# One matmul chain for group 1, its loads' issuers and the start's filler matmuls rearranged in an S5 and MLP kernel

## The chip, the cores and the metric

The kernel runs on one core of a Trainium2 chip. The metric is the device time of one execution in microseconds (us), as the median of several runs. The engines are named as in the profile: PE (TensorE), PEld (its weight loads), ACT (ScalarE), DVE (VectorE), POOL (GpSimd) and SP (SyncE, which issues DMAs).

## The reference

x is 2048 rows of 448 columns in bf16. A layer norm of x feeds two branches: a diagonal complex state space model (S5), and an MLP behind a second layer norm, whose silu gates the first.

```python
xn = layernorm(x)
# S5: 448 complex states, one recurrence over the 2048 rows
Lam_bar = exp(dt * Lam);  B_bar = ((Lam_bar - 1) / Lam)[:, None] * B
Bu = xn @ B_bar.T
for t in range(2048):
    h = Lam_bar * h + Bu[t]          # hs[t] = h
s = 2 * real(hs @ C.T) + xn * Dskip
# MLP 448 -> 1792 -> 448
m = gelu(layernorm(xn) @ w1 + b1) @ w2 + b2
out = x + s * silu(m)
```

## The kernel before

The rows are worked in four groups of 512. For each group the kernel makes both norms, transposes them by DMA (`xn` to `xnT`, `xn2` to `xn2T`), forms the MLP's first product with w1 (`mm1_phase`, matmuls of L662, gelus of L668 on ACT into `gT`), its second with w2 (`mm2`, L784 and L787, silu of L790), the state inputs (`bu_phase`, L691: rows are taken in pairs, so each group has 256 columns of two rows), the scan of the states (`ssm`, L740 to L769, with the scans themselves at L750, the states of odd and even rows in `hx` and `hz`), the output of the state space model (`yt`, L806 to L829), and the sum that is written out (`out_dma`, or `out_pe` for the last group). Group 0 also makes its tables: decay powers in `WT`, the scaled B and C matrices (`BT`, `CQ`, `CZ`; L596, L597).

Nothing is issued where it is written. Each operation is recorded as a task with the keys that it reads and writes; `link()` derives what it must wait for from the order in which the tasks are written; `emit()` then issues all tasks in the order of a list of numbers, ORDER (L154). Each engine works through its own instructions in that order, and waits on semaphores. Some tasks have two forms, for two engines (a copy on ACT or DVE, a small operation on POOL or DVE, a row of a norm on DVE or ACT, the four numbers of a norm's scale on POOL or DVE: ten DVE instructions L423 to L433, or five POOL ones with a power): a second list, SECOND (L174), names the tasks that take the second form.

The written order, from which the dependencies come, is a string of words, STEPS (L180). `m1211` is the first product (m) of group 1, tile pair 2, on bank pair 1, second phase (1); a tile pair is two times 128 of the 1792 columns, phase 0 takes three quarters of its depth, phase 1 the rest, and the gelus follow phase 1. `b0031` is a state input of group 0, job 0, bank pair 3, stage 1. `W` is a tile of the second product, `S` a scan, `Y` an output, `L` and `N` norms, `G` and `U` the gelu and the silu table's load on ACT (L466). The bank pairs of PSUM are 0 and 1, 2 and 3, 4 and 7, 5 and 6.

At the start, x, w1 (four chunks, each a main part of three times 128 rows and a remainder of 64 rows, `ldw1`), B and w2 are loaded by SP's queue, the parameters of the states and b1 by ACT's. PE runs filler matmuls on constants (`dummies`, L378) between its first small matmuls, then turns b1 and the skip row into columns (L549, L555), and begins group 0's first product (L662), which runs in halves of 256 columns. The product needs `xn2T` of group 0, whose halves come from PE transposes (L407) by copies (L301), and the w1 chunk with its remainder; the copy of the 64 rows at L301 or L302 within `w1_sb` is needed by a second phase.

Of the kernel before, what the change touches and what calls it, by code (L numbers as in the profile page):

```python
# [148 lines left out]
def dram_ap(t, offset, ap):  # L149
    return bass.AP(tensor=t.tensor, offset=offset, ap=ap)  # L150
# [1 line left out]


ORDER = [int(k) for k in """  # L154
# [18 lines left out]
""".split()]  # L173
SECOND = [int(k) for k in """  # L174
26 29 32 56 60 69 83 90 113 115 172 173 175 177 178 180 181 182 202 204 205 207 208 209 210 212 214 216 218 220 222 234 236 238 240 244 246 256 258
270 277 278 280 324 338 349 360 361 364 365 409 443 444 445 446 471 472 473 474 475 487 489 527 528 529 542 549 551 560 575
""".split()]


STEPS = """  # L180
L1 N1 W006 W015 W022 W033 G1 m1000 m1120 m1001 m1210 m1121 m1300 m1211 m1301 m1410 b0030 m1500 b0120 m1411 b0031 b0121 m1501 b0032 m1610 b0122 m1611
b0033 b0123 U1 L2 S0 W130 W101 W112 W123 G2 m2000 m2110 b1020 m2001 m2111 b1130 m2200 b1021 m2310 m2201 b1131 m2311 m2400 b1022 m2510 b1132 m2401
m2511 b1023 m2600 b1133 m2601 U2 L3 Y03d2 Y00d3 Y01d4 Y02d7 O0 N2 S1 W205 W216 W220 W231 Y13d2 Y10d3 Y11d4 Y12d7 O1 N3 G3 m3000 b2030 m3110 b2120
m3001 b2031 m3111 b2121 m3200 b2032 m3310 b2122 m3201 b2033 m3311 b2123 S2 m3400 b3030 m3510 b3120 m3401 b3031 b3121 m3511 b3032 m3600 b3122 m3601
# [13 lines left out]
def bass_recurrent_scan__ssm_conv_s5__mixer_channel_mlp__prompt_kernel(  # L198
# [11 lines left out]
    L, D, F = 2048, 448, 1792  # L210
# [6 lines left out]
    with ExitStack() as es:  # L217
        def SB(name, shape, dtype=BF):
            return es.enter_context(nc.sbuf_tensor(name, shape, dtype))
# [12 lines left out]
        w1_sb = SB("w1_sb", [128, 4, F])  # L232
# [9 lines left out]
        drows = vrows[64:66, 64:512]  # L242
# [54 lines left out]
        def pe(fn, reads=(), writes=(), split=False):  # L297
            kb.add("pe", fn, reads, writes, split=split)

        def copy(pairs, rd, wr):  # L300
            kb.either(("act", [lambda e, o=o, i=i: e.activation(o, i, ACT.Copy) for o, i in pairs]),  # L301
                      ("dve", [lambda e, o=o, i=i: e.tensor_copy(o, i) for o, i in pairs]), rd, wr)  # L302

        with nc.Block():
# [17 lines left out]
            def ld(eng, o, i, writes, reads=()):  # L322
                kb.dma(eng, o, i, reads=reads, writes=writes)
# [4 lines left out]
            def ldx(b0, n, reads=()):  # L328
                ld("sp", x_all[:, b0:b0 + n, :, :], dram_ap(A_x, b0 * 256 * D, [[2 * D, 128], [256 * D, n], [D, 2], [1, D]]),
                   [f"x{b}" for b in range(b0, b0 + n)], reads)  # L330
# [4 lines left out]
            def ldw1(c):  # L335
                a, w = CH[c][0] * 128, CH[c][1] * 128
                ld("sp", w1_sb[:, 0:3, a:a + w], dram_ap(B_w1, a, [[F, 128], [128 * F, 3], [1, w]]), [f"w1_{c}"])
                ld("sp", w1_sb[64:128, 3, a:a + w], dram_ap(B_w1, 384 * F + a, [[F, 64], [1, w]]), [f"w1r_{c}"])
                copy([(w1_sb[0:64, 3, a:a + w], w1_sb[64:128, 2, a:a + w])], [f"w1_{c}"], [f"w1c_{c}"])

            for par in range(2):
                ld("sp", x_all[:, 0, par, :], dram_ap(A_x, par * D, [[2 * D, 128], [1, D]]), [f"x0p{par}"])
            ldx(1, 1)
            ldw1(0)
            ld("act", brows[0:3, :], dram_ap(B_b1, 256, [[512, 3], [1, 512]]), ["br0"], ["br"])
            ld("act", brows[3:4, 0:256], dram_ap(B_b1, 0, [[256, 1], [1, 256]]), ["br1"], ["br"])
            for c in range(1, 4):
                ldw1(c)
# [3 lines left out]
            for c, (a, n) in enumerate(CH):  # L352
                ld("sp", w2_sb[:, a:a + n, :], dram_ap(B_w2, a * 128 * D, [[n * D, 128], [D, n], [1, D]]), [f"w2_{c}"])
            for i, vec in enumerate((A_Dskip, B_b2)):
                ld("sp", drows[i:i + 1, :], dram_ap(vec, 0, [[D, 1], [1, D]]), [f"dbr{i}"])
            ldx(2, 2)
            def xk(b):
                return [f"x{b}"] if b else ["x0p0", "x0p1"]
# [17 lines left out]
            def dummies(n, rd=(), bank=3, cols=256):  # L376
                wide = nc.const_aps.tensor_like(1.0, xn_sb[:, 0, 0:cols])
                pe([lambda e: e.matmul(psum[:, bank, 0:cols], one, wide, start=True, stop=True) for _ in range(n)], list(rd), [f"ps{bank}"])  # L378
# [169 lines left out]
            def b1_columns():  # L548
                pe([lambda e, k=k: e.matmul(psum[:, 4, 2 + k:11 + k:4], brows[0:4, k:512:4], ident[32:36, 32:35], start=True, stop=True) for k in range(4)]  # L549
                   + [lambda e, k=k: e.matmul(psum[:, 4, k:k + 1], brows[0:4, k:256:2], ident[32:36, 35:36], start=True, stop=True) for k in range(2)],  # L550
                   ["br", "br0", "br1", "ident"], ["ps4"])
                copy([(b1f[:], psum[:, 4, 0:14])], ["ps4"], ["b1f"])
# [119 lines left out]
            def mm1_run(g, b, js, pairs):  # L672
                for j in js:
                    mm1_phase(g, b, j, pairs[j - js[0]], False)
                    if j > js[0]:
                        mm1_phase(g, b, j - 1, pairs[j - 1 - js[0]], True)
                mm1_phase(g, b, js[-1], pairs[js[-1] - js[0]], True)
# [205 lines left out]
            dummies(1, ["st0"])  # L883
            first_apply(0)
            b1_columns()
            mm1_run(0, 0, range(6), (0, 1, 2, 0, 1, 2))
            first_apply(1)
            mm1_run(0, None, range(6, 7), (0,))
# [83 lines left out]
```

## Time and profile before

| | |
|---|---|
| median of 3 runs | 148.27 us (147.64 to 148.87) |
| profiled execution | 148.68 us |
| its span, from first to last instruction | 146.9 us |
| mean granted clock of PE over the span | 0.984 |
| PE busy | 140.0 us (95%) |
| DVE busy | 130.7 us (89%) |
| ACT busy | 102.8 us (70%) |
| POOL busy | 23.9 us (16%) |

Times in the views are in microseconds from the start of the span, and 1.78 us of the profiled execution lie outside it. A row of a chain or a timeline gives start, length, engine, line and operation, then how many instructions it groups; in brackets stands the idle time ahead of it with what ended it. A granted clock of 1.00 is PE's full speed.

### The profile page before, as it was taken

To read this page: it belongs to the slowest core of one execution; us is meant where nothing else is said; L and a number is where in the kernel's file an instruction comes from. 1 tells how busy PE (TensorE), PEld (TensorE's weight loads), DVE (VectorE), ACT (ScalarE), POOL (GpSimd) and SP (SyncE) were. 2 spreads that over 40 slices of the span, in tenths; PEclk is the share of its full clock that TensorE was granted. 3 is DMA by queue.
4 is the path that set the end of the run, shared out by engine and by line. 5 is a ranking of instruction groups with operands and counts; after the bars stand their busy time and mean duration, and the time that the engine had idled before them with its cause. 6 is when DMAs were issued, how large, how long until landed. Compare 5 with 4: busy or idle time off the path is not lost.

```text
span 146.9 us, 3570 instructions
## 1 busy us (share of the span) xinstructions
PE 140.0 (95%) x1421; PEld 90.2 (61%) x1427; DVE 130.7 (89%) x284; ACT 102.8 (70%) x188; POOL 23.9 (16%) x83
## 2 busy tenths in 40 slices
PE   7789999999999999999999999999999999999990
PEld 2577774454455485466758555887775668564860
DVE  2989999999587999999999999496999999999891
ACT  3667999988799766999989773615768997064200
POOL 2630777710000000060500000000000600000000
PEclk9977999999999999999999999999999999999998
DMA  4799996999589791000000018917440010005404
GB/s 114 219 253 275 393 230 127 167 251 184 105 170 230 146 112 35 2 4 0 4 0 0 0 22 160 212 38 147 84 155 0 0 63 4 18 0 107 182 10 125
DMA packets 38850, 15.98 MB, mean 109 GB/s; under 512 B 33193, under 2 KB 38450, under 8 KB 38834
## 3 DMA queue, kind: packets, MB, share of 16 engines
q1 hardware_dynamic: 38276, 15.52, 47.6%
q10 hardware_dynamic: 558, 0.24, 0.6%
q8 instruction: 11, 0.18, 0.5%
q14 instruction: 5, 0.04, 0.1%
HBM read 5.86 MB, written 1.84 MB: 52 GB/s over the span
## 4 chain that ended last, share of the span: by engine, by line
PE 86%; ACT 4%; SPq 2%; DMA 2%; issue 1%; DVE 1%; DVEq 0%
PE psum L662 28%; PE psum L784 24%; PE psum L691 14%; PE psum L806 7%; PE psum L807 6%; PE psum L787 4%; ACT gT L668 3%; SPq L78 2%; DMA w_sb<-in_B_w_dram 2%; PE psum L814 2%; ACT xn_sb L444 1%; DVE Bn L862 1%; ACT tmp L595 0%; PE psum L815 0%; PE psum L856 0%
## 5 line engine op out<-in xcount | busy, mean ns | idle before, releaser
L662 PE MATMUL psum<-xn2T,w_sb 64*128 64x512 bf16 (+1 forms) x476 | 48.3, 349 | 0.7 <-DMA w_sb<-in_B_w_dram 0.4
L668 ACT ACTIVATE gT<-psum,b1f 128x512 bf16<-128x512 f32 (+1 forms) x68 | 37.3, 615 | 4.9 <-PE psum L662 3.9
L784 PE MATMUL psum<-gT,w_sb 128*128 128x512 bf16 x162 | 36.3, 379 | 0.6 <-issue 0.3
L662 PEld LDWEIGHTS psum<-xn2T,w_sb 64*128 64x128 bf16 x476 | 26.5, 111 | 16.6 <-PE psum L662 1.9
L784 PEld LDWEIGHTS psum<-gT,w_sb 128*128 128x128 bf16 x168 | 16.2, 98 | 18.9 <-issue 0.6
L691 PE MATMUL psum<-xnT,BT 64*128 64x256 bf16 x392 | 24.4, 269 | 0.0
L691 PEld LDWEIGHTS psum<-xnT,BT 64*128 64x128 bf16 x392 | 18.8, 94 | 6.2 <-issue 0.8
L790 ACT ACTIVATE g_sb<-psum,db 128x512 bf16<-128x512 f32 (+1 forms) x16 | 9.8, 627 | 10.2 <-PE psum L787 4.6
L750 DVE TENSOR_TENSOR_SCAN s_w<-vs,dk 128x1048 f32<-128x1048 bf16 (+1 forms) x8 | 16.4, 2061 | 0.2
L444 ACT ACTIVATE xn_sb<-x_all,lnw 128x448 bf16<-128x448 bf16 (+2 forms) x20 | 13.2, 696 | 0.1
L827 DVE SCALAR_TENSOR_TENSOR tmp<-xnT,db,psum 128x512 f32<-128x512 bf16 (+1 forms) x17 | 10.8, 650 | 2.5 <-PE psum L815 1.8
L301 ACT ACTIVATE vs<-s_w 64x258 bf16<-64x258 f32 (+2 forms) x11 | 6.5, 611 | 6.7 <-DVE s_w L750 6.6
L806 PE MATMUL psum<-hx,CZ 128*128 128x256 bf16 x84 | 10.9, 275 | 0.0
L807 PE MATMUL psum<-Bn,CQ 128*128 128x256 bf16 x84 | 10.8, 273 | 0.0
L466 ACT ACT_TABLE_LOAD x8 | 10.3, 1283 | 0.3
L301 ACT ACTIVATE ue<-psum 128x512 bf16<-128x512 f32 (+1 forms) x14 | 7.1, 548 | 4.5 <-PE psum L691 4.5
L806 PEld LDWEIGHTS psum<-hx,CZ 128*128 128x128 bf16 x84 | 8.0, 98 | 2.4 <-ACT u_sb L301 0.4
L807 PEld LDWEIGHTS psum<-Bn,CQ 128*128 128x128 bf16 x84 | 8.0, 98 | 1.6 <-issue 0.4
L829 DVE TENSOR_TENSOR t<-tmp,g_sb 128x512 bf16<-128x512 f32 (+1 forms) x14 | 8.4, 626 | 0.0
L301 ACT ACTIVATE u_sb<-psum 128x256 bf16<-128x256 f32 (+1 forms) x14 | 6.1, 508 | 2.8 <-PE psum L691 2.8
L443 DVE TENSOR_SCALAR xn_sb<-x_all,lnw 128x384 bf16<-128x384 bf16 (+2 forms) x20 | 6.1, 353 | 1.8 <-ACT xn_sb L444 1.7
L364 DVE BATCH_NORM_STATS2 lnst<-x_all 128x6 f32<-128x448 bf16 x12 | 7.0, 614 | 0.0
(158 smaller groups left out, 174.4 us busy)
## 6 DMA issues: line engine op xcount, KB each, us to landing
x_all<-in_A_x_dram SPq DMA_DIRECT2D x3, 448.0 KB, 4.7
w_sb<-in_B_w_dram SPq DMA_DIRECT2D x3, 448.0 KB, 7.1
out_dram<-Bn SPq DMA_DIRECT2D x6, 224.0 KB, 2.9
w_sb<-in_B_w_dram SPq DMA_DIRECT2D x3, 384.0 KB, 4.3
Bn<-in_A_B_im_dram SPq DMA_DIRECT2D x1, 336.0 KB, 7.6
Bn<-in_A_B_re_dram SPq DMA_DIRECT2D x1, 336.0 KB, 7.9
x_all<-in_A_x_dram SPq DMA_DIRECT2D x2, 112.0 KB, 2.1
x_all<-in_A_x_dram SPq DMA_DIRECT2D x1, 224.0 KB, 2.6
```

The lines of the kernel that those rows point to most:

```text
L301: kb.either(("act", [lambda e, o=o, i=i: e.activation(o, i, ACT.Copy) for o, i in pairs]), ("dve", [lambda e, o=o, i=i: e.tensor_copy(o, i ...
L444: ("act", [lambda e, o=o, i=i: e.activation(o, i, ACT.Identity, bias=nb, scale=rs) for o, i in parts]),
L466: kb.add("act", lambda e: e.preload_act_table_set(what), reads, writes, sem=name)
L662: return lambda e: e.matmul(dst(bk[k]), w1_sb[rows, d, fcol(2 * j + k)], rhs[rows, d], start=not second and n == 0, stop=second and n == 3)
L668: act(lambda e, k=k, fi=fi: e.activation(gT[:, gb, fi, cols], psum[:, bk[k], cols], ACT.Gelu_apprx_tanh, bias=b1f[:, fi:fi + 1]), ["b1f", ...
L691: fns.append(lambda e, rows=rows, bank=bank, m=m, o=o, n=n: e.matmul(psum[:, bank, c * NK:(c + 1) * NK].rearrange("p (b c) -> p b c", b=2) ...
L750: dve(lambda e, so=so, vi=vi, di=di: e.tensor_tensor_scan(so, vi, di, 0.0, ALU.add, ALU.mult), ["v", "vl", "vz", "dk", "dk01"] + ["v3"] * ...
L784: pe([lambda e, fi=fi: e.matmul(psum[:, bk, :], w2_sb[:, fi, 128 * j:128 * j + 128], gT[:, gb, fi, :], start=fi == 0, stop=fi == NF - 1) f ...
L790: act(lambda e: e.activation(g_sb[:, gb, 512 * j:512 * j + n], psum[:, bk, 0:n], ACT.Silu, bias=b2c[:, j:j + 1]), [f"ps{bk}", "db", f"Ws{g ...
L806: pe([lambda e, k=k: e.matmul(par(psum[:, bk, :], 1), CZ[:, k, cols], halves(hx[:, hb, k, 1:NK + 1]), start=k == 0, stop=k == 6) for k in ...
L807: fns = [lambda e, k=k: e.matmul(par(psum[:, bk, :], 0), CQ[:, k, cols], halves(hz[:, hb, k, :]), start=not by_pe and k == 0, stop=not by_ ...
L827: dve([lambda e, o=o, p=p, x=x, d=d: e.scalar_tensor_tensor(out=v(o), in0=x, scalar=d, in1=v(p), op0=ALU.mult, op1=ALU.add) for o, p, x, d ...
```

## The change

Five things are edited. In STEPS group 1's first product is written as one chain of words on three bank pairs (0, 1 and 2), where its pairs 4 to 6 used pairs 0 and 1 in turn with group 0's state inputs between them; the state inputs follow behind. ORDER and SECOND are new. The loads of w1's remainders are issued by ACT instead of SP. The loads of the skip row and of b2 are issued by POOL instead of SP. Three filler matmuls of 512 columns are written behind `b1_columns()`.

```diff
 ORDER = [int(k) for k in """
-9 11 16 17 18 44 14 15 13 42 24 10 22 12 4 23 360 2 93 94 95 96 97 106 0 101 1 45 92 105 107 46 47 98 111 49 41 99 102 25 50 19 20 100 66 27 34 110 3
...
+14 0 44 1 5 15 2 13 45 92 362 16 17 18 11 24 19 12 4 3 6 9 7 93 22 94 105 96 97 95 106 101 23 98 111 99 41 42 46 66 25 102 107 100 108 109 20 27 47 67
...
 STEPS = """
-L1 N1 W006 W015 W022 W033 G1 m1000 m1120 m1001 m1210 m1121 m1300 m1211 m1301 m1410 b0030 m1500 b0120 m1411 b0031 b0121 m1501 b0032 m1610 b0122 m1611
+L1 N1 W006 W015 W022 W033 G1 m1000 m1120 m1001 m1210 m1121 m1300 m1211 m1420 m1301 m1510 m1421 m1600 m1511 m1601 b0030 b0120 b0031 b0121 b0032 b0122
 b0033 b0123 U1 L2 S0 W130 W101 W112 W123 G2 m2000 m2110 b1020 m2001 m2111 b1130 m2200 b1021 m2310 m2201 b1131 m2311 m2400 b1022 m2510 b1132 m2401
...
             def ldw1(c):
                 a, w = CH[c][0] * 128, CH[c][1] * 128
                 ld("sp", w1_sb[:, 0:3, a:a + w], dram_ap(B_w1, a, [[F, 128], [128 * F, 3], [1, w]]), [f"w1_{c}"])
-                ld("sp", w1_sb[64:128, 3, a:a + w], dram_ap(B_w1, 384 * F + a, [[F, 64], [1, w]]), [f"w1r_{c}"])
+                ld("act", w1_sb[64:128, 3, a:a + w], dram_ap(B_w1, 384 * F + a, [[F, 64], [1, w]]), [f"w1r_{c}"])
...
             for i, vec in enumerate((A_Dskip, B_b2)):
-                ld("sp", drows[i:i + 1, :], dram_ap(vec, 0, [[D, 1], [1, D]]), [f"dbr{i}"])
+                ld("pool", drows[i:i + 1, :], dram_ap(vec, 0, [[D, 1], [1, D]]), [f"dbr{i}"])
...
             b1_columns()
+            dummies(3, cols=512)
             mm1_run(0, 0, range(6), (0, 1, 2, 0, 1, 2))
```

On PE, the engine that works through the products, these are the rows from group 0's second product (the first L784) to the middle of group 2's first product (L662 behind the state inputs, L691), before:

```order
L784 MATMUL psum<-gT,w_sb 128x512 x42
L787 MATMUL psum<-gT,w_sb 64x256 x28
L662 MATMUL psum<-xn2T,w_sb 128x512 x90
L691 MATMUL psum<-xnT,BT 128x256 x12
L662 MATMUL psum<-xn2T,w_sb 128x512 x8
L691 MATMUL psum<-xnT,BT 128x256 x16
L784 MATMUL psum<-gT,w_sb 128x512 x26
L691 MATMUL psum<-xnT,BT 128x256 x34
L787 MATMUL psum<-gT,w_sb 64x256 x28
L691 MATMUL psum<-xnT,BT 128x256 x36
L784 MATMUL psum<-gT,w_sb 128x512 x16
L662 MATMUL psum<-xn2T,w_sb 128x512 x6
```

The same place on PE now, with group 1's second product in one piece behind its first (the second L784):

```order
L784 MATMUL psum<-gT,w_sb 128x512 x42
L787 MATMUL psum<-gT,w_sb 64x256 x28
L662 MATMUL psum<-xn2T,w_sb 128x512 x98
L784 MATMUL psum<-gT,w_sb 128x512 x42
L787 MATMUL psum<-gT,w_sb 64x256 x28
L691 MATMUL psum<-xnT,BT 128x256 x56
L662 MATMUL psum<-xn2T,w_sb 128x512 x6
L691 MATMUL psum<-xnT,BT 128x256 x12
L662 MATMUL psum<-xn2T,w_sb 128x512 x8
L691 MATMUL psum<-xnT,BT 128x256 x30
```

Group 0's 98 state-input matmuls, which lay among group 1's first and second products, now come behind both, with 14 of group 2's first product between them.

On ACT, the rows of the start before, from the first norm's Ln (L388) to the load of the gelu table (L466); `w_sb` here is w1, `xn2T<-psum` is the copy of a transposed half:

```order
L388 ACTIVATE lnw<-lnmv,eps 128x1
L389 ACTIVATE lnw<-lnw 128x1
L301 ACTIVATE xn2T<-psum 128x512
L485 ACTIVATE cw<-cw 128x8
L392 ACTIVATE lnw<-lnmv,eps 128x2
L393 ACTIVATE lnw<-lnw 128x2
L301 ACTIVATE w_sb<-w_sb 64x256
L466 ACT_TABLE_LOAD
```

The same place on ACT now, with the issues of w1's remainders among them (L78, DMA):

```order
L388 ACTIVATE lnw<-lnmv,eps 128x1
L389 ACTIVATE lnw<-lnw 128x1
L478 ACTIVATE cw<-psum 128x12
L78 DMA w_sb<-in_B_w_dram 64x512
L78 DMA w_sb<-in_B_w_dram 64x256
L479 ACTIVATE cw<-cw 128x4
L78 DMA w_sb<-in_B_w_dram 64x512 x2
L392 ACTIVATE lnw<-lnmv,eps 128x2
L393 ACTIVATE lnw<-lnw 128x2
L301 ACTIVATE xn2T<-psum 128x512
L485 ACTIVATE cw<-cw 128x8
L466 ACT_TABLE_LOAD
```

Four DMA issues and the second pair of Ln and Exp moved ahead of the copy of xn2T; the copy within w1 left ACT for DVE.

On DVE, the rows of group 0's scan (from L741 to the sum of the states, L766) before:

```order
L741 TENSOR_TENSOR pb<-u_sb,WT 128x6x256
L740 TENSOR_TENSOR pa<-u_sb,WT 128x6x256
L742 TENSOR_TENSOR vs<-pa,pb 128x3x2x256
L743 TENSOR_TENSOR pa<-u_sb,WT 128x2x256
L368 BN_AGGR lnmv<-lnst 128x2
L744 TENSOR_TENSOR vs<-pa 128x256
L750 SCALAR_TENSOR_TENSOR s_w<-vs,dk 128x1048
L368 BN_AGGR lnmv<-lnst 128x2
L302 CAST vs<-s_w 128x258
L302 CAST vs<-s_w 64x258 x2
L750 SCALAR_TENSOR_TENSOR s_w<-vs,dk 128x786
L714 TENSOR_TENSOR u_sb<-psum,ue 128x256
```

The same place on DVE now:

```order
L741 TENSOR_TENSOR pb<-u_sb,WT 128x6x256
L740 TENSOR_TENSOR pa<-u_sb,WT 128x6x256
L742 TENSOR_TENSOR vs<-pa,pb 128x3x2x256
L743 TENSOR_TENSOR pa<-u_sb,WT 128x2x256
L750 SCALAR_TENSOR_TENSOR s_w<-vs,dk 128x786
L744 TENSOR_TENSOR vs<-pa 128x256
L750 SCALAR_TENSOR_TENSOR s_w<-vs,dk 128x1048
L714 TENSOR_TENSOR u_sb<-psum,ue 128x256
L597 SCALAR_TENSOR_TENSOR CQ<-Cr,cw,tmp 128x448
L302 CAST vs<-s_w 128x258
L302 CAST vs<-s_w 64x258 x2
```

The two scans (L750) changed places, and two sums of norm statistics (L368) lie elsewhere; behind these rows the wide cast of the states (`vs<-s_w 128x3x2x258`) and one L596 are no longer DVE's.

More of the change, by code (lines that the diff above doesn't have):

```diff
@@ L154 @@
 ORDER = [int(k) for k in """
[18 rows of a table removed]
[18 rows of a table added]
 """.split()]
 SECOND = [int(k) for k in """
-26 29 32 56 60 69 83 90 113 115 172 173 175 177 178 180 181 182 202 204 205 207 208 209 210 212 214 216 218 220 222 234 236 238 240 244 246 256 258
-270 277 278 280 324 338 349 360 361 364 365 409 443 444 445 446 471 472 473 474 475 487 489 527 528 529 542 549 551 560 575
+21 26 29 32 48 50 51 57 59 63 64 66 71 72 73 79 90 110 115 173 175 177 179 181 203 208 209 210 211 213 215 217 219 221 223 237 241 245 247 251 253 255
+257 271 274 278 281 326 329 332 337 353 354 366 444 446 447 472 473 474 475 476 528 529 530 531 532 543 550 552 561 576 579
 """.split()]
 STEPS = """
-L1 N1 W006 W015 W022 W033 G1 m1000 m1120 m1001 m1210 m1121 m1300 m1211 m1301 m1410 b0030 m1500 b0120 m1411 b0031 b0121 m1501 b0032 m1610 b0122 m1611
+L1 N1 W006 W015 W022 W033 G1 m1000 m1120 m1001 m1210 m1121 m1300 m1211 m1420 m1301 m1510 m1421 m1600 m1511 m1601 b0030 b0120 b0031 b0121 b0032 b0122
 b0033 b0123 U1 L2 S0 W130 W101 W112 W123 G2 m2000 m2110 b1020 m2001 m2111 b1130 m2200 b1021 m2310 m2201 b1131 m2311 m2400 b1022 m2510 b1132 m2401
```

34 rows, old and new, of the table ORDER are left out of this document.

## The prediction

> **What bounds the kernel now.** I began with the page's busy slices, which say which engine is full and at what clock TensorE (PE) runs.
>
> ```profile
> span 146.9 us, 3570 instructions
> PE   7789999999999999999999999999999999999990
> DVE  2989999999587999999999999496999999999891
> PEclk9977999999999999999999999999999999999998
> ```
>
> PE is full from the fifth slice of 3.7 us to the last but one, and VectorE (DVE) nearly so from the third. PE's clock is below full in slices three and four, that is from about 7 to 15 us. Next the chain of waits in order of time (start, length, link):
>
> ```profile
> 4.67 3.47 DMA w_sb<-in_B_w_dram
> 8.27 4.48 PE psum L662 x48
> ...
> 12.80 5.69 PE psum L662 x84
> ...
> 18.53 3.03 PE psum L662 x50
> ...
> 21.73 9.01 PE psum L784 x41
> ...
> 30.74 1.65 PE psum L787 x28
> ...
> 32.39 6.22 PE psum L662 x55
> ...
> 38.63 1.26 ACT gT L668 x2
> ...
> 45.32 5.56 PE psum L784 x25
> ...
> 54.49 2.07 PE psum L691 x36
> ...
> 73.27 3.02 PE psum L662 x28
> ```
>
> The end is set by matmuls one behind the other. A transfer of w1 that lands at 4.67 + 3.47 = 8.14 releases the first product at 8.27; group 0's second product follows (21.73), then group 1's first product (32.39), in which the chain once passes to ScalarE's (ACT's) gelus, then group 1's second product (45.32), with group 0's state inputs (L691) ending at 54.49 + 2.07 = 56.56. Third, busy time by stretch (stretch, length, then PE, PEld, DVE, ACT, POOL, granted clock, DMA share, GB/s):
>
> ```profile
> 7.00:8.00 1.00, 0.33 (x5) 0.25 (x5) 0.97 (x5) 0.61 (x2) 0.70 (x3) 1.00 0.76 233
> 9.00:10.00 1.00, 1.00 (x16) 0.90 (x14) 0.82 (x5) 0.22 (x2) 0.83 (x4) 0.59 0.80 211
> 10.00:11.00 1.00, 1.00 (x12) 0.90 (x10) 0.84 (x5) 0.70 (x2) 0.04 (x1) 0.50 1.17 250
> 32.39:45.32 12.93, 12.64 (x126) 6.43 (x128) 10.50 (x33) 11.55 (x19) 0.00 (x0) 1.00 0.85 164
> 57.23:135.98 78.75, 78.58 (x809) 51.17 (x810) 74.07 (x112) 55.90 (x100) 7.33 (x14) 1.00 0.23 48
> ```
>
> PE does a third of a microsecond of work in 7 to 8, and soon after its clock is granted at half. From 57.23, the first state scan's start, to 135.98, where the last group's h is ready, PE waits 0.17 us and DVE 4.68 us of 78.75. So two engines are close to full there: a microsecond that PE gains earlier reaches the end only if DVE keeps up.
>
> **The start: w1's remainders on ACT.** Eight transfers of w1 and two of the skip rows leave SP's queue in part: the four remainders go to ACT, the rows of skip and b2 to GpSimd. What an issue costs, and what stands on ACT and PE there:
>
> ```profile
> 3.41 2.40 SPq L78 DMA_DIRECT2D w_sb<-in_B_w_dram  x4
> 3.78 1.03 PE L378 MATMUL psum<-const-bfloat16-1.0 128*128 128x256 bf16 x4
> 4.93 0.20 ACT L389 ACTIVATE lnw<-lnw 128x1 f32<-128x1 f32 x1
> 5.54 0.60 ACT L301 ACTIVATE xn2T<-psum 128x512 bf16<-128x512 bf16 x1 [0.41 <-PE psum L407]
> 7.50 0.21 PE L555 MATMUL psum<-ident,dk 2*128 2x2 bf16 x3 [0.86 <-issue]
> 143.24 1.31 ACTq L78 DMA_DIRECT2D out_dram<-Bn  x2
> w_sb<-in_B_w_dram SPq DMA_DIRECT2D x1, 32.0 KB, 3.5
> out_dram<-Bn ACTq DMA_DIRECT2D x1, 128.0 KB, 2.3
> ```
>
> An issue takes 2.40/4 = 0.60 us on SP and 1.31/2 = 0.65 on ACT. ACT's order puts four of them between its second Exp (done by about 5.1) and its copy of the transposed xn2T, which ran at 5.54. Four are 2.5 us, so the copy runs at about 8.04 and ends at 8.64; PE's skip columns reuse the bank that it reads (0.21 us), and the product begins at 8.85 in place of 8.27. If the wait for the second norm's Ln and Exp, now ahead of the copy, doesn't overlap, it is 0.4 later. The remainder itself goes out at about 5.6, 0.9 later than before's 4.67; landing after 2.3 (ACT's writes at the end) or 3.5 (SP's load here) gives 7.9 to 9.1. I take 8.85, bounds 8.27 (nothing late) and 9.3. The page "DMA: Bandwidth & Descriptors" of the Trainium skill, under "Issuing engines are not separate DMA queues", says that transfers of all issuing engines run on the same sixteen DMA engines, so that another issuer saves sequencer time alone; by it the landing stays at 3.5 and the product begins at about 9.2. The trace of before has no load of ACT's under this traffic to say so. What SP gains, 4 × 0.60, pulls later chunks of w1, which nothing in the chain waits for. The skip rows are needed by L555 too. GpSimd issues them among its first settings; no row has an issue of its own, so I take SP's and ACT's 0.60 to 0.65 for each and 3.5 to land: issued by 4, they are there by 7.5 and cost nothing.
>
> **The dummies.** Three 512-column matmuls go ahead of the skip columns. Four of 256 took 1.03 us at half clock, so three are 1.55 at half and 0.8 at full clock, which was granted in 7 to 8: they fit in the 0.86 us that PE idled before L555, and cost nothing as long as the copy is what the product waits for. Whether they keep the clock is the unknown. Group 0's first product is 168 matmuls of 256 columns and 14 of 512; at full clock one of 256 takes 3.03/50 = 0.0606 us and one of 512 takes 3.02/28 = 0.108, in all 10.18 + 1.51 = 11.69. It took 18.53 + 3.03 − 8.27 = 13.29, so half clock cost 1.6 us; that is the gain's upper bound, and 0 its lower one. The gap that remains until 8.85 is longer than before's, and the dummies fill about as much as it grew, so I call it even, with a slight lean to held: the filled share of 6 to 9 us rises by 0.8. Held, the product takes 11.69, but then the gelus bind:
>
> ```profile
> 9.86 0.84 ACT L668 ACTIVATE gT<-psum,b1f 128x256 bf16<-128x256 f32 x2 [0.78 <-DVE w_sb L302]
> 7.80 1.28 ACT L466 ACT_TABLE_LOAD   x1
> ```
>
> The gelu table (1.28) now follows the copy: 8.64 + some small work + 1.28 is 10.1, and 14 pairs of gelus at 0.84 end at 21.9; PE's last phase comes a pair earlier, at 20.9 to 21.0. With the 0.17 to 21.73 as before and 9.01 + 1.65 for the second product, group 1's first product begins at T = 31.7 (before 32.39). With the clock lost as before, T = 8.85 + 13.29 + 0.17 + 10.66 = 33.0.
>
> **Group 1's chain.** In before, 98 matmuls (10.57 us at 0.108) and 28 of L691 at 2.07/36 = 0.0575 (1.61) filled 12.93 us: up to 0.75 was lost to gelus between which ACT had other work. Now 98 stand alone, with three pairs of banks in place of two, and ACT has 14 pairs' worth of gelus behind one another; I take no loss (bounds 0 and 0.75). Then 10.66 for the second product. The 98 matmuls of group 0's state inputs (5.63), with 14 of group 2's first product between them (1.51), come after. So the inputs are done at T + 10.57 + 10.66 + 5.63 + 1.51 = T + 28.4, where before they were done at 56.56 − 32.39 = 24.2 after the same point: 4.2 later against the start of the group, 3.5 later on the clock. PE's sum is only reordered; DVE gets its first scan late. With 57.23 − 56.56 = 0.67 for the last copy, it begins at 31.7 + 28.4 + 0.67 = 60.8.
>
> **What DVE has to make up.** Rows of the stretch from the first scan:
>
> ```profile
> 57.23 0.96 DVE L741 TENSOR_TENSOR pb<-u_sb,WT 128x1536 bf16<-128x1536 bf16 x1 [0.17 <-ACT u_sb L301]
> 66.88 1.23 DVE L302 CAST vs<-s_w 128x1548 bf16<-128x1548 f32 x1
> 68.39 0.68 DVE L597 SCALAR_TENSOR_TENSOR CQ<-Cr,cw,tmp 128x448 bf16<-128x448 bf16 x1
> 93.60 0.97 DVE L827 SCALAR_TENSOR_TENSOR tmp<-xnT,db,psum 64x256 f32<-64x256 bf16 x2 [1.77 <-PE psum L815]
> 100.72 0.69 DVE L302 CAST ue<-psum 128x512 bf16<-128x512 f32 x1 [0.84 <-PE psum L691]
> 135.69 0.29 DVE L768 TENSOR_TENSOR hx<-pa 128x258 bf16<-128x258 bf16 x1
> ```
>
> DVE waits 1.77 and 0.84 for PE there. With DVE 3.5 later and PE earlier those 2.61 go. The order also takes work out of the stretch: the cast of 1.23 goes to ACT, one L597 (0.68) falls before the first scan, and some ten small ones (statistics' sums, copies of half a tile) move ahead of it or to GpSimd; bounded by L768's 0.29 each, 0 to 2.9, I take 1.4. In all 3.3. New waits, where a late DVE hands to PE and back, I put between 0 and the old 2.61, half: 1.3. So 78.75 − 2.61 − 3.3 + 1.3 = 74.1, and h of the last group is ready at 60.8 + 74.1 = 134.9 (before 135.98). PE alone needs 135.98 − 32.39 − 0.75 = 102.8 from T, 134.5: DVE is last by 0.4. What follows (10.9 us to the end) is unchanged. The span falls by 1.1. The profiled execution of 148.68 (146.9 of span, 1.78 around it) becomes 147.6; it lies 0.41 above the median 148.27, so the median becomes **147.2**.
>
> **Rivals.** A, held clock and nothing late: the product begins at 8.27, the gelus keep pace, T = 8.27 + 11.69 + 0.17 + 10.66 = 30.8, and DVE makes up all: PE is last at 133.6, 2.4 earlier: 145.9. For it: DVE's row shows waits enough to fill. Against: the four issues ahead of ACT's copy.
>
> C, the change doesn't do what it says: the clock falls all the same, T = 33.0; the scan begins at 62.1, h is ready at 136.2: 148.5. For it: in before PE's longest pause between 6 and 9 us is 0.86, and the clock still fell, so what makes it fall isn't plainly a pause that three dummies close. The Trainium skill, "TensorE: Matmul & The Clock Gate", under "What's actually happening", has the clock fall after an idle window of 3.4 us that runs free of the kernel, so that its place varies between runs; the 0.50 granted after pauses of 0.86 doesn't agree with idleness of a whole window, and by that rule the dummies would buy nothing.
>
> B, slower: group 2's transposed xn2T comes late.
>
> ```profile
> 50.89 1.78 SPq L77 DMA_TRANSPOSE xn2T<-xn_sb  x1
> xn2T<-xn_sb SPq DMA_TRANSPOSE x4, 4.7
> ```
>
> It was issued at 50.89 and takes 4.7 to land, 55.6. In the new order six of group 2's matmuls stand between the first and second half of group 0's state inputs, at T + 10.57 + 10.66 + 56 × 0.0575 = T + 24.4 = 56.1. If DVE reaches that norm later than 51.4, each microsecond delays the state inputs behind them and the first scan. At 3.3 later than before (54.2) the wait is 2.8, the scan begins at 63.6, h is ready at 137.7: +1.7, 150.0. For it: DVE gets the sine chain, casts of u's neighbours and a w1 copy ahead of that point; against: one of its two long scale chains goes to GpSimd there, and half the norm's rows to ACT.
>
> **How the numbers follow.** Forecast 0.40 (own range 146.4 to 148.0), A 0.26, C 0.16, B 0.18. About 1% is what a measurement of this kernel tells from no change: 146.8 and 149.75. A is faster in full (0.26), and a quarter of the forecast's range (0.10): faster 0.36. The rest of the forecast (0.30), C (0.16) and B with a short wait (0.03) are the same: 0.49. Slower 0.15. The range runs from 145.4 (A with another half microsecond from the clock's later windows) to 149.5, which leaves out A's end and the longer waits of B.
>
> **What would show it.** Right: first L662 near 8.85; clock at full in slices three and four; no ACT link in group 1's product; first scan near 60.8 and 74 us from there to the last L768. Wrong: clock rows at 0.50 near 10 (C); PE waiting on a DMA into xn2T near 56 (B); the first L662 at 8.3 (A); and, against all four, a stretch from the first scan as long as before's 78.75, which would put the end at 150 or later.

## The result: slower by 2.8%

The changed kernel takes 152.0 us as the median of four runs (151.48 to 152.96), the kernel before 147.95 beside it: a ratio of 1.028, 95% interval 1.0227 to 1.0334. The forecast was 147.2, its range 145.4 to 149.5. The profiled execution is 152.39 us with a span of 150.7, 3.8 more than before's 146.9. The page's lines of the slices, after the change:

```profile
span 150.7 us, 3565 instructions
PE   7669999999999999999999999998999999999990
DVE  2759299799896987999998999796999999999881
PEclk9965999999999999999999999999999999999997
```

PE's second and third slices are down to 6, where before had 7 and 8, and its clock is down to 5 tenths in the fourth. The chain of waits of the changed kernel (start, length, link) says how long the start lasts:

```profile
5.41 5.41 DMA w_sb<-in_B_w_dram
10.82 0.14 issue
10.95 5.05 PE psum L662 x48
...
24.98 9.01 PE psum L784 x41
33.99 1.65 PE psum L787 x28
35.64 6.86 PE psum L662 x62
...
42.55 4.08 PE psum L662 x36
...
46.78 9.15 PE psum L784 x41
```

The remainder of w1's first chunk is out on ACT at 5.41 and lands 5.41 later, at 10.82. The first product begins at 10.95 instead of 8.27. The timeline of PE, ACT and SP (start, length, what, and in brackets the idle time ahead) shows a second load that is late, and what stands in front of both:

```profile
2.20 2.03 SPq L78 DMA_DIRECT2D w_sb<-in_B_w_dram  x4
...
4.12 0.23 ACTq L78 DMA_DIRECT2D dk<-in_B_b_dram  x1
...
8.57 0.27 PE L549 MATMUL psum<-ident,dk 4*128 4x3 bf16 x4 [2.46 <-DMA dk<-in_B_b_dram]
...
8.82 1.46 PE L378 MATMUL psum<-const-bfloat16-1.0 128*128 128x512 bf16 x3
```

SP, freed of the remainders and of the two rows that GpSimd now issues, issues all four main parts of w1 by 4.23. b1's second row, which before's order issued at 2.24, now stands on ACT behind the first Ln and Exp, goes out at 4.12 and holds PE's L549 until 8.57. The windows of the changed kernel (stretch, length, then PE, PEld, DVE, ACT, POOL, clock, DMA share, GB/s) have the DMA engines full and PE idle from 7 to 8, and the engines nearly idle from 9 on, when the remainder has not landed yet:

```profile
7.00:8.00 1.00, 0.00 (x0) 0.00 (x0) 0.00 (x0) 0.62 (x3) 0.46 (x3) 1.00 1.06 371
8.00:9.00 1.00, 0.43 (x7) 0.39 (x8) 0.08 (x1) 0.37 (x1) 0.00 (x0) 0.88 0.84 200
9.00:10.00 1.00, 1.00 (x3) 0.15 (x1) 0.94 (x6) 0.21 (x1) 0.00 (x0) 0.50 0.17 30
10.00:11.00 1.00, 0.63 (x8) 0.35 (x9) 0.94 (x4) 0.99 (x1) 0.79 (x3) 0.50 0.04 13
...
14.00:15.00 1.00, 1.00 (x14) 0.78 (x12) 0.90 (x5) 0.35 (x2) 0.80 (x3) 0.50 0.81 296
65.00:139.17 74.17, 73.52 (x776) 48.76 (x776) 70.30 (x103) 54.31 (x98) 6.99 (x11) 1.00 0.28 54
```

The last row is DVE's stretch from the first scan to the last group's h, between these two instructions of its timeline:

```profile
65.00 0.96 DVE L741 TENSOR_TENSOR pb<-u_sb,WT 128x1536 bf16<-128x1536 bf16 x1 [0.16 <-ACT u_sb L301]
...
138.88 0.29 DVE L768 TENSOR_TENSOR hx<-pa 128x258 bf16<-128x258 bf16 x1
...
144.55 0.69 DVE L829 TENSOR_TENSOR t<-psum,g_sb 128x512 bf16<-128x512 f32 x1 [0.49 <-PE psum L809]
```

So the 3.8 us divide in four. Group 1's first product begins at 35.64 instead of 32.39: +3.25. From there to the first scan 29.36 instead of 24.84: +4.52. The stretch to the last h 74.17 instead of 78.75: −4.58. The end behind it 11.5 instead of 10.9: +0.6. The middle two, which lie behind the start and hold the moved chain, cancel. What is left is the start and, far smaller, the end. Of the start's 3.25, 2.68 are the product's later beginning (10.95 for 8.27), and the rest is its longer time (13.87 for 13.29), more of it at half clock. The lost clock is not what makes the loss: of the four runs the longest, 152.96, had a mean clock of 0.993.

### The profile page after: what moved, and what is told of

The parts are those of the page before. It is cut to its first block, busy times and chain, and to the rows that moved or that the text cites. A ratio compares the mean times of both kernels' runs of the same rounds, so it can differ in the third digit from the quotient of the medians.

```text
span 150.7 us, 3565 instructions
## 1 busy us (share of the span) xinstructions
PE 141.7 (94%) x1425; PEld 90.9 (60%) x1430; DVE 128.8 (86%) x274; ACT 105.4 (70%) x191; POOL 27.8 (18%) x82
## 4 chain that ended last, share of the span: by engine, by line
PE 85%; DMA 5%; DVE 5%; issue 2%; ACT 0%; DVEq 0%; ACTq 0%
PE psum L662 31%; PE psum L784 24%; PE psum L691 14%; PE psum L806 6%; PE psum L807 5%; PE psum L787 4%; DMA w_sb<-in_B_w_dram 4%; DVE t L829 2%; DVE tmp L827 1%; DMA x_all<-in_A_x_dram 1%; PE psum L814 1%; DVE lnst L385 1%; DVE Bn L862 0%; DVE lnmv L386 0%; DVEq L304 0%
## 5 line engine op out<-in xcount | busy, mean ns | idle before, releaser
L662 PE MATMUL psum<-xn2T,w_sb 64*128 64x512 bf16 (+1 forms) x476 | 48.6, 352 | 0.6 <-DMA w_sb<-in_B_w_dram 0.4
L784 PE MATMUL psum<-gT,w_sb 128*128 128x512 bf16 x163 | 36.1, 379 | 0.6 <-issue 0.5
L662 PEld LDWEIGHTS psum<-xn2T,w_sb 64*128 64x128 bf16 x476 | 27.0, 112 | 15.9 <-PE psum L662 1.2
L784 PEld LDWEIGHTS psum<-gT,w_sb 128*128 128x128 bf16 x168 | 16.1, 98 | 19.7 <-ACT gT L668 0.9
L691 PE MATMUL psum<-xnT,BT 64*128 64x256 bf16 x392 | 24.2, 269 | 0.4 <-DVE tmp L827 0.4
L691 PEld LDWEIGHTS psum<-xnT,BT 64*128 64x128 bf16 x392 | 18.8, 94 | 6.2 <-DVE tmp L827 0.7
L750 DVE TENSOR_TENSOR_SCAN s_w<-vs,dk 128x786 f32<-128x786 bf16 (+1 forms) x8 | 16.3, 2056 | 0.0
L301 ACT ACTIVATE vs<-s_w 64x258 bf16<-64x258 f32 (+2 forms) x12 | 8.2, 687 | 6.5 <-DVE s_w L750 6.5
L827 DVE SCALAR_TENSOR_TENSOR tmp<-xnT,db,psum 128x512 f32<-128x512 bf16 (+1 forms) x17 | 10.8, 648 | 1.6 <-PE psum L807 1.4
L301 ACT ACTIVATE ue<-psum 128x512 bf16<-128x512 f32 (+1 forms) x12 | 6.1, 542 | 4.2 <-PE psum L691 4.0
L787 PE MATMUL psum<-gT,w_sb 128*64 128x256 bf16 x112 | 6.9, 274 | 0.0
L443 DVE TENSOR_SCALAR xn_sb<-x_all,lnw 128x448 bf16<-128x448 bf16 (+2 forms) x18 | 5.9, 358 | 1.0 <-ACT xn_sb L444 0.9
```

The costliest lines, as they stand in the source:

```text
L662: return lambda e: e.matmul(dst(bk[k]), w1_sb[rows, d, fcol(2 * j + k)], rhs[rows, d], start=not second and n == 0, stop=second and n == 3)
L691: fns.append(lambda e, rows=rows, bank=bank, m=m, o=o, n=n: e.matmul(psum[:, bank, c * NK:(c + 1) * NK].rearrange("p (b c) -> p b c", b=2) ...
L750: dve(lambda e, so=so, vi=vi, di=di: e.tensor_tensor_scan(so, vi, di, 0.0, ALU.add, ALU.mult), ["v", "vl", "vz", "dk", "dk01"] + ["v3"] * ...
L784: pe([lambda e, fi=fi: e.matmul(psum[:, bk, :], w2_sb[:, fi, 128 * j:128 * j + 128], gT[:, gb, fi, :], start=fi == 0, stop=fi == NF - 1) f ...
L787: pe([lambda e, fi=fi, r=r: e.matmul(halves(psum[64 * r:64 * r + 64, bk, 0:NK]), w2_sb[:, fi, 384:D], par(gT[:, gb, fi, :], r), start=fi = ...
L827: dve([lambda e, o=o, p=p, x=x, d=d: e.scalar_tensor_tensor(out=v(o), in0=x, scalar=d, in1=v(p), op0=ALU.mult, op1=ALU.add) for o, p, x, d ...
```

## The experiments

Each is compared with the kernel before on the same chip. "Q" is the theory that the remainders are late because the main parts fill the DMA engines ahead of them.

**The remainders back on SP.**

```diff
-                ld("act", w1_sb[64:128, 3, a:a + w], ...
+                ld("sp", w1_sb[64:128, 3, a:a + w], ...
 # and in ORDER each remainder right behind its main part
```

> The changed kernel, but w1's four remainders are issued by SP again, each right behind its main part, as the first eight transfers after x. Everything else, b1's second row and the dummies included, as in the changed kernel. Theory Q (the remainders land late because all four main parts, issued ahead of them, fill the DMA engines): the first remainder goes out at about 3.8 us and lands by 7.5, so the first product no longer waits for it; it then waits for b1's second row (issued at 4.1 on ACT, landing near 8) and the work behind it and begins near 9.5 instead of 10.95: 150.5 us. Rival R (ACT's own queue sets the start, its copy of xn2T would be late anyway): with the issues gone the copy runs near 6, and the start is the same 9.5, but the first remainder would not be seen landing earlier. Rival N (the start is not what costs the time): no change from 152.0.

Measured 148.3 us, ratio 1.0008 (0.9967 to 1.0049): with the issuer and these places in the order alone, no loss is left that the runs can tell. PE's timeline:

```profile
8.45 0.83 PE L662 MATMUL psum<-xn2T,w_sb 64*128 64x256 bf16 x12
9.62 4.74 PE L662 MATMUL psum<-xn2T,w_sb 64*128 64x256 bf16 x70 [0.35 <-DVE w_sb L302]
```

The product begins at 8.45, even with b1's row where the change put it; that row, too, came earlier here, at 7.03, 3.03 after its issue. The expectation had the start a microsecond too late because it kept the row's landing at 8. N falls. The run can't tell Q from R, since it takes the issues from ACT as well.

**b1's second row early.**

```diff
-18 11 24 19 12 4 3 6 9 7 93 22 94 105 96 97 95 106 101 23 98
+18 11 24 19 12 4 3 6 9 7 93 22 23 94 105 96 97 95 106 101 98
```

> The changed kernel, but ACT issues b1's second row right behind its first rows, ahead of the first Ln and Exp, as before's kernel did. Theory Q: b1's matmuls (L549) run near 6.2 instead of 8.57, so PE's pause of 2.46 us goes, but the first product still begins near 10.9, when the remainder of w1 has landed: the time stays at 152.0 less at most 0.6, what a second window of half clock cost. Rival I (it is PE's pause behind b1's row that delays the product): the product begins near 9 and the time falls to about 150.

Measured 152.15 us, ratio 1.0281 (1.0217 to 1.0345): no change. L549 ran at 6.56, and the product still began at 10.98; the first remainder, out at 5.40, landed 5.4 later. (The trace names a copy of DVE's, done at 10.85, as what released the product; the product's first phase in the kernel needs no such copy, but it does need the remainder, which landed at about 10.8.) I falls as an account of its own.

**No dummies in the changed kernel.**

```diff
-            dummies(3, cols=512)
+            dummies(1, cols=2)
```

> The changed kernel, with the three dummies of 512 columns replaced by one matmul of 2 columns. Theory Q: the product waits for the transfer, so the dummies' 1.46 us cost nothing and hold no clock that was not lost already: 152.0, product at 10.95. Rival D (the dummies delay the product): the product begins up to 0.7 earlier: 151.3. Rival H (the dummies shorten the time at half clock): without them the product stays longer at half clock, and the time rises by up to 1.7.

Measured 151.27 us, ratio 1.024 (1.0174 to 1.0307), which overlaps the changed kernel's interval: no difference that these runs can tell. The time is the one that D forecast, and in the profile the product does begin earlier, at 9.93. But there the remainder landed sooner (4.36 after its issue) and PE waited 1.06 us for it, so the dummies were not what the product waited for. Why it landed sooner in that execution stays open. H falls for the changed kernel: the time doesn't rise without the dummies, which there stand at 8.82, behind the clock's fall (0.50 from 8.75).

**Only the issuer, in the kernel before.**

```diff
-                ld("sp", w1_sb[64:128, 3, a:a + w], ...
+                ld("act", w1_sb[64:128, 3, a:a + w], ...
 # ORDER, SECOND and STEPS as before
```

> The kernel before, with one edit: w1's remainders are issued by ACT, at the places that its own order gives them. Theory Q: SP's main parts of w1 move up, the first remainder goes out behind ACT's second Exp (about 5.2) and lands near 10, so the first product begins near 10.2 instead of 8.27 and the time rises from 148 to about 150. If only the changed kernel's order matters (rival O), the time stays within 0.5 of before's.

Measured 151.99 us, ratio 1.0271 (1.0217 to 1.0326): the same loss without any other part of the change. The chain of this kernel:

```profile
5.64 5.63 DMA w_sb<-in_B_w_dram
11.27 0.14 issue
11.41 4.87 PE psum L662 x48
```

ACT's order puts the first remainder at 5.64, behind the second Exp, and it lands 5.63 later. Here b1's row was early, the xn2T copy done at 6.9, and PE idle for 3.74 us. O falls. The loss was near 4 us where I had expected 2: the landing took 5.6 where I had put 4.8, and the clock was at half from 8.83 to 15.66.

**Early remainders on ACT.**

```diff
-4 3 6 9 7 93 22 94 105 96 97 95 106 101 23 98 111 99 41 42 46 66 25 102 107 100 108 109 20 27
+4 3 6 9 7 93 22 25 20 94 105 96 97 95 106 101 23 98 111 99 41 42 46 66 102 107 100 108 109 27
```

> The changed kernel, but ACT issues the remainders of w1's first two chunks right behind b1's first rows, near 2.3 us, beside SP's main parts and not behind them. Theory Q (what costs is that the remainders reach the DMA engines behind 1.3 MB of main parts, whoever issues them): they land by about 7, the first product waits for b1's second row and the dummies and begins near 9.0; with group 1's product T near 32.3 the time is 148.8. Rival A (a transfer that ACT issues is slow by itself, because its queue gets a small share beside SP's): it still lands 4.4 to 5.4 us after its issue, near 7.5, and the time is the same or 0.5 more; then e6 tells them apart.

Measured 151.55 us, ratio 1.0242 (1.0188 to 1.0297). The remainder was out of the way, because it went out early: its landing still took 4.5 us, as rival A has it. But b1's row, issued at 4.24, now set the start, as the chain shows:

```profile
4.24 4.22 DMA dk<-in_B_b_dram
...
8.91 1.39 PE psum L378 x3
...
10.61 3.50 PE psum L662 x45
```

The row of half a kilobyte took 4.22 us. Behind it the dummies ran at half clock and were on the path here. So the two late loads hid behind each other: mending either one alone gives nothing that these runs can tell. The expected 148.8 was wrong because I took the row to land by 8 and the dummies at full clock.

**Two main parts held back.**

```diff
-                ld("sp", w1_sb[:, 0:3, a:a + w], ..., [f"w1_{c}"])
+                ld("sp", w1_sb[:, 0:3, a:a + w], ..., [f"w1_{c}"], ["w1_0"] * (c > 1))
```

> The changed kernel, with one edit: SP holds the main parts of w1's last two chunks until chunk 0's main part has landed. ACT issues the remainders as late as in the changed kernel (4.8 and 5.4 us). Theory Q: with two main parts out of the way the first remainder lands 2.5 to 3.5 us after its issue, near 8.5, and the first product begins near 9.0 in place of 10.95: about 150.0, or 0.5 more if the held parts come too late for the product's later phases. Rival A (ACT's transfers are slow by themselves, or its late issue alone is what costs): landing stays at 10.8 and the time at 152.0.

Measured 148.1 us, ratio 1.0026 (0.9998 to 1.0054). ACT issues at 4.84 and 5.44, as late as in the changed kernel. The row of the DMA view for the first chunk's remainder (KB, us to landing) in the changed kernel:

```profile
w_sb<-in_B_w_dram ACTq DMA_DIRECT2D x1, 32.0 KB, 5.4
```

The same row of this kernel:

```profile
w_sb<-in_B_w_dram ACTq DMA_DIRECT2D x1, 32.0 KB, 2.3
```

And the product in its timeline of PE:

```profile
8.81 11.67 PE L662 MATMUL psum<-xn2T,w_sb 64*128 64x256 bf16 x182
```

The same transfer, from the same queue and at the same time, lands in 2.3 us instead of 5.4 when 768 KB of main parts aren't in front of it; the other two parts (576 KB) were issued ahead of it in both kernels. That is Q, shown, and A falls. It also fits the windows of the changed kernel: 10.82 less 2.3 is 8.5, an estimate of when the remainder's turn came, and the engines' share falls between 8 and 10. R holds only as the next bound: ACT's late copy of xn2T (from 7.83) lets the product begin at 8.81, not at 10.95. The time came out 1.9 lower than expected. The clock stayed at 0.994 or more in all ten runs, which the expectation had not counted on, and the chain shows no wait for a held part.

**The start mended in five places.**

```diff
+ # remainders on SP behind their main parts, chunk 0 first
+ # ORDER: 23 behind 22; 113 ahead of 103; 172 behind 119
```

> The changed kernel with its start mended in five places: remainders on SP, each behind its main part, chunk 0 first; b1's second row issued behind its first; ACT's copy of xn2T ahead of the second pair of Ln and Exp; the skip columns' matmuls behind the first three phases of the product. Group 1's chain, the dummies and the rest as changed. The product should begin near 7.4 in place of 10.95 (8.45 in e1). If DVE's stretch from the first scan to the last group's h is again 74.2, every microsecond at the start is one at the end: 147.3, about 0.9 less than before. Rival V (with the start earlier DVE's or ACT's own work ahead of the first scan is what sets it): no faster than e1, 148.3.

Measured 148.72 us, ratio 1.0067 (1.0035 to 1.01). The product does begin at 7.07, but then waits in its own first phases:

```profile
8.05 0.52 PE L662 MATMUL psum<-xn2T,w_sb 64*128 64x256 bf16 x6 [0.47 <-DMA w_sb<-in_B_w_dram]
9.55 0.61 PE L662 MATMUL psum<-xn2T,w_sb 64*128 64x256 bf16 x8 [0.99 <-DVE w_sb L302]
```

DVE's copy of chunk 0's rows stands behind a copy that waits for chunk 1 and behind the second norm. Group 1's first product began at 31.79. That is V.

**The dummies alone, in the kernel before.**

```diff
             b1_columns()
+            dummies(3, cols=512)
             mm1_run(0, 0, range(6), (0, 1, 2, 0, 1, 2))
```

> The kernel before with one edit: the three dummies of 512 columns ahead of the skip columns. If they keep the clock at full through group 0's product (the forecast's lean), that product takes 11.7 us in place of 13.3 and the time falls by up to 1.5 to about 146.8 where before lost its clock, by less where it had kept it. If the clock falls all the same (rival C), 148.2. If they delay the product: 148.5.

Measured 147.53 us, ratio 0.9977 (0.9948 to 1.0005). The granted clock was 0.993 or more in all twelve runs, so the dummies do hold it. In the profiled execution, which at 148.64 us was the longest of the twelve, a row of PE's timeline says where the gain went:

```profile
14.42 7.12 PE L662 MATMUL psum<-xn2T,w_sb 64*128 64x512 bf16 x106 [1.57 <-DMA xn2T<-xn_sb]
```

PE, faster, waits 1.57 us for the transposed second half of xn2T, and group 1's first product begins at 32.36, as without dummies. Whether the shorter runs waited as long, no trace shows. The kernel before isn't always at half clock there either. Of the 84 runs of it that these ratios rest on, 36 had a mean clock below 0.99, with a median of 148.27 us, and 48 had 0.99 or more, with 147.46.

**The dummies, and the second half earlier.**

```diff
 # e8, and in ORDER DVE's copy of chunk 1's rows (26) behind the norm of xn2T's second half
```

> The kernel before with two edits: the three dummies (as in e8, where PE kept full clock but then waited 1.57 us for the transposed second half of xn2T, landed at 14.37), and DVE's copy of w1's rows of chunk 1 behind the norm of that second half instead of ahead of it, where it held DVE until 6.8 for a transfer. If that wait is where the held clock's gain went, the transpose is issued about 0.7 earlier, group 1's first product begins near 31.7 in place of 32.36, and the time falls by 0.7 against e8: 146.9. If the transpose's landing isn't moved (other traffic sets it), 147.5 as e8.

Measured 147.53 us, ratio 0.9977 (0.9949 to 1.0005), no better than e8. In its profile the wait for xn2T is gone and group 1's first product begins at 31.47, but that execution also started late (its x arrived at 3.94, and its three dummies took 1.46 us where e8's took 0.82), and group 1's chain then ran through ACT's gelus from 37.69 to 44.31. Before's chain runs through the same gelus. Whether they or the run's late start took the gain stays open.

**Held main parts with four more moves.**

```diff
 # e6, and in ORDER: 23 behind 22; 113 and 103 ahead of 28 and 31; the last instructions in before's order
```

> The changed kernel with main parts held as in e6, and four moves: b1's second row issued behind its first; ACT's copy of xn2T and the second Ln and Exp ahead of the last two chunks' remainders; the order of DVE's and PE's last instructions as in before's kernel (e6 lost 0.55 us behind the last L768 against before, to two waits of DVE for PE of 0.49 and 0.57). Theory: the product begins near 7.5 to 8 instead of 8.88, so 0.8 off if DVE's 74.2 us from the first scan is unchanged, and 0.4 off at the end: 146.9. Rival V (the start is set by DVE's copies and norms, as in e7): only the end's 0.4: 147.7.

Measured 148.27 us, ratio 1.0047 (1.0022 to 1.0071): neither the expected 146.9 nor V's 147.7. The product began at 7.61, but the third chunk's remainder, moved behind the copy, was out at 6.96 into the main parts that had then been released, and landed 4.61 later:

```profile
6.96 4.61 DMA w_sb<-in_B_w_dram
...
11.67 0.53 PE psum L662 x6
```

It is the same fault as the change's, two chunks on, and my own move made it.

**Both small loads early, all on ACT.**

```diff
-4 3 6 9 7 93 22 94 105 96 97 95 106 101 23 98 111 99 41 42 46 66 25 102 107 100 108 109 20 27
+4 3 6 9 7 93 22 23 25 20 94 105 96 97 95 106 101 98 111 99 41 42 46 66 102 107 100 108 109 27
```

> The changed kernel, with all of ACT's early transfers together: b1's second row and then the remainders of the first two chunks right behind b1's first rows; SP's queue as changed. In e2 the row came early and the product waited for the remainder (10.85); in e5 the remainder came early and the product waited for the row (landed 8.46). Theory Q: each hid behind the other; with both early the product begins near 8.5 and the time falls to about 148.5. Rival A (transfers of ACT's queue are held back by SP's full queue whenever they are issued): the start stays past 9.5 and the time above 150.

Measured 147.92 us, ratio 1.0006 (0.9976 to 1.0036). Three numbers moved in ACT's order undo the loss, with the issuer, SP's queue, the chain and the dummies as changed. The first remainder's landing took 4.0 us here, far more than e6's 2.3, but it was issued before 3.8. So A falls here as well: the start is early enough, though the transfer is not short. The start of group 0's product in PE's timeline:

```profile
8.33 7.92 PE L662 MATMUL psum<-xn2T,w_sb 64*128 64x256 bf16 x116
```

Group 1's first product begins at 31.06.

**The same, with before's order at the end.**

```diff
 # e11, and behind the last group's h the instructions of DVE and PE in before's order
```

> e11 (b1's second row and the remainders of the first two chunks early on ACT) with the order of the last instructions of DVE and PE, behind the last group's h, as in before's kernel. In e11 the span ends 11.5 us behind the last L768, in before 10.9; DVE waits there 0.57 and 0.49 for PE. If the order is why, the end comes 0.4 to 0.5 earlier: 147.5, a shade under before's 147.98 (ratio 0.997). If it is the transfers out that set the end, no change from e11's 147.92.

Measured 147.56 us, ratio 0.9972 (0.9937 to 1.0007), the fastest with the chain in it, and still not told from the kernel before. In its profile the last L768 ends at 134.31 and the span at 145.4, 11.1 behind it; e11 had 11.5. DVE's 0.49 wait for L809 is gone, so the order of the last instructions was worth about 0.4 of the 0.6. The chain of this profile begins at another load that the change moved, the row of b2 that GpSimd issues, which PE's L555 needs:

```profile
3.60 4.17 DMA dk<-in_B_b_dram
...
7.86 0.21 PE psum L555 x3
```

With the two late loads on ACT mended, this third one sets the start in this profile.

## Why the prediction was wrong

**What bounded the kernel** was read rightly: PE's chain from the first product on, with DVE close behind, and no slack behind either, so that the 3.25 us lost at the start were lost at the end.

**The start is the step that failed.** It put the product at 8.85 (bounds 8.27 and 9.3); it began at 10.95. The prediction made two faults there. First, it priced the remainder's landing at 2.3 to 3.5 us, from a write at the end of the kernel and from before's own load, which had two main parts issued ahead of it and not four, and it wrote that the later chunks of w1, which SP's freed time pulls forward, were something "which nothing in the chain waits for". Nothing waits for them, but the remainders now queue behind them: 5.41 us, and 2.3 with two of the four parts held (e6). The issuer alone, in the kernel before, makes the same loss (e4). Second, it read ACT's order for what stands ahead of the copy of xn2T and missed that b1's second row had moved behind an Ln and an Exp too. PE's 2.46 us at L549, after which the clock fell (at 8.75), come from it: they stay in e5 (2.44) and are gone in e2 and e11. The wait for the remainder costs the clock by itself too, since in e2 it was at half from 9.80 on. The copy of xn2T, on which the term was built, did run late as worked out (7.79 to 8.37, forecast 8.04 to 8.64), and set nothing. A third load was priced too low without harm here: the rows that GpSimd issues took 4.2 and 4.5 us to land, not 3.5, the second from 3.60 to about 8.1, and it is what e12's start waits for.

The Trainium skill, in "DMA: Bandwidth & Descriptors" under "Issuing engines are not separate DMA queues", spoke against the move, and the runs agree: one more issuer bought nothing. But its price as I took it, a landing of 3.5 and a start near 9.2, was too low: the landing was 5.4 to 5.6 in the changed kernel, e2 and e4, and 4.4 in e3, with the engines' share at 1.06 from 7 to 8 in the changed kernel.

**The dummies** cost nothing that e3 can tell in the changed kernel, as said. That they would hold the clock is right where no long pause comes first: it was 0.993 or more in every run of e8 and e6, and 0.995 and 1.00 in the profiled runs of e1 and e11. With it falls the reading under C by which the dummies would buy nothing for the clock. The four of 256 columns that the prediction calls "at half clock" stand under a granted clock of 1.00 (3.78 to 4.81); the price came out all the same, 1.46 us for the three at 0.50 and 0.82 at 1.00 (e8). In the changed kernel the pause came ahead of them. The clock of 0.50 lasted from 8.75 to 15.58, and the product took 13.87 us instead of the forecast's 11.7. With the start mended group 1's first product began at T = 31.06 to 31.45 (e11, e6, e1); the forecast had 31.7.

**Group 1's chain** to the first scan was forecast at 29.1 from T and took 29.36. No loss had been taken, and the 98 matmuls lost 0.4 (35.64 to 46.62, for 10.57 at full pace), the second product 0.3 more; the state inputs and the last copy gave 0.4 back.

**DVE's stretch** was forecast at 74.1 and took 74.17 in the changed kernel, e1 and e6. Two of its terms missed and cancelled: work left by 3.77 (70.30 busy, from 74.07) where I had 3.3, and waiting fell by 0.81 where I had 1.3. That the sum came out within 0.1 is luck, then. The gain that it was to bring at the last h is there when the start is mended: 134.58 in e11, for the forecast's 134.9 and before's 135.98.

**The end**, taken as unchanged, cost 0.6, two thirds of it by the order of PE's and DVE's last instructions (e12). And before's median is a mix of runs with and without the clock lost: a held clock was worth 0.2 at the median (e8), which the runs don't tell from nothing, and not the 1.6 of its profile. So even with the start mended, e11 and e12 are not shown to be faster than before.

**The rivals.** B had the right side and the wrong place: PE didn't wait for group 2's xn2T in any of these chains. C's first half happened, T late and the clock down, far past its price: 35.64 where C had 33.0 and before 32.39. What C and the forecast both lacked was a load that waits in the DMA engines. A's start came with e11 (the product at 8.33, T 31.06 for A's 30.8), but not A's 145.9: DVE didn't make up all, with the last h at 134.58 for A's 133.6, and the end cost more.

## What to carry to other kernels

A transfer that is moved to an idle queue has to be placed by when it reaches the DMA engines, and all that the old queue will now issue sooner counts as standing ahead of it. A small load that gates a chain goes out first, on whatever engine: it may still land slowly (4.0 to 4.5 us in e5 and e11), but in time. Where two late loads hide behind each other, mending one shows nothing. In a diff of an order, each engine's first dozen rows are to be read in full, every DMA among them, not only those around the one that was asked about.

## What was not expected of the hardware

A transfer of 32 KB landed 2.1 to 2.3 us after its issue with two main parts of w1 issued ahead of it and two held back (e10, e6). It took 3.0 to 3.5 in SP's queue behind the same two (e8, e9, the kernel before), and 4.4 to 5.6 behind all four (e3, e2, the changed kernel, e4), though it came from another engine's queue. Issued by ACT among the main parts, it took 4.0 to 4.5 (e11, e12, e5). A row of 0.5 KB took 4.2 (e5).

PE's half clock lasted 3.41 us in the kernel before (9.16 to 12.57) and in e5 (8.69 to 12.10), and twice that in the changed kernel (8.75 to 15.58) and in e4 (8.83 to 15.66) and e2 (9.80 to 16.63). So in these traces it is given back in steps of 3.41. Here are the changed kernel's stretch of that length ahead of the fall and its two stretches at half clock:

```profile
5.34:8.75 3.41, 0.95 (x15) 0.72 (x13) 1.38 (x7) 1.19 (x4) 1.04 (x8) 1.00 1.03 321
8.75:12.16 3.41, 3.04 (x25) 1.61 (x24) 3.09 (x13) 1.49 (x2) 0.79 (x3) 0.50 0.12 23
12.16:15.58 3.42, 3.42 (x36) 2.71 (x32) 2.78 (x9) 1.62 (x4) 1.97 (x4) 0.50 1.04 251
```

It fell behind a stretch with PE busy for 0.95 of 3.41 us here, and for 2.10 in the kernel before (5.75 to 9.16). With 3.04 of 3.41 busy it wasn't given back; with 3.42 of 3.42 it was, and with 3.36 in e2 (13.21 to 16.63). Where between 3.04 and 3.36 the line lies, no run here tells. And the clock's row doesn't tell all: under a granted 1.00 the three dummies took 1.46 us in e9 and 0.82 in e8.
